# Gating the second pair of hardware loads on the first, and reordering the first software loads, in a windowed-attention plus feed-forward kernel

## The chip, the core and the metric

The kernel runs on one core of a Trainium2 chip. The metric is device time in microseconds (us) of one execution. Every kernel is executed several times and the median is quoted. One further execution is taken with the hardware profiler on; its times are counted in us from the start of the profiled span.

The engines are named as the profile names them: PE multiplies matrices, PEld is its loading of the stationary operand, DVE is the vector engine, ACT the scalar engine, POOL the general-purpose engine, SP the synchronisation engine. Each works through its own list of instructions in the order in which they were written. DMA transfers can be issued by SP and ACT ("hardware" queues q1 and q10 in the profile) and by POOL ("software" queue q0, the only one of the three that is used here to change float32 to bfloat16 on the way). All of them are carried out by the same 16 DMA engines.

## What is computed

The reference, cut to what matters: attention in a window of 32 positions to either side, over 8 batches, 8 heads, 576 positions and 64 columns per head, and behind it two matrix products with a squared ReLU between them.

```python
B, H, S, D = 8, 8, 576, 64
scores = np.matmul(q, k.transpose(0, 1, 3, 2)) / np.sqrt(D)
pos = np.arange(S)
mask = np.abs(pos[:, None] - pos[None, :]) <= 32
scores = np.where(mask, scores, -1e9)
scores = scores - np.max(scores, axis=-1, keepdims=True)
attn = np.exp(scores)
attn = attn / (np.sum(attn, axis=-1, keepdims=True) + 1e-09)
x = np.matmul(attn, v).transpose(0, 2, 1, 3).reshape(B * S, H * D)   # 4608 x 512
r = np.maximum(x @ w_in, 0.0)                                        # 4608 x 2048
out = (r * r) @ w_out                                                # 4608 x 512
```

## The kernel before

The work is cut into 72 attention steps of 64 tokens (nine per batch, numbered n) and nine feed-forward tiles of 512 tokens. For an attention step PE multiplies the keys around the 64 tokens with the queries (`scores`), ACT takes the exponential, DVE multiplies with the mask, PE multiplies with V (`av`), DVE divides by the sum (`evac`), and PE turns the result so that the columns lie on the partitions (`xturn`; later batches use a DMA transpose of SP for that). ACT copies the turned block into XT. When four groups of 128 tokens are there, the feed-forward of a tile can run: `mm1_small` and its larger relatives multiply with a quarter of the first weight (W1), ACT applies ReLU, DVE squares, and `mm2` multiplies with the second weight (W2).

**How the order comes about.** Nothing is issued directly. Every operation is recorded with the tags that it reads and writes, a planned duration, a `key` that serves as priority and, for a DMA, a planned amount of transfer (`move`). `schedule` then plans the five engines several times with a model of the engines and the DMA queues, keeps the plan with the best planned end, and `emit` writes each engine's instructions in that order with the semaphore waits that the tags ask for. An operation with a key of -100 or less keeps that key in every plan. A small change of keys or of planned transfer times therefore changes the written order of PE, DVE, ACT and SP far beyond the place of the edit.

**Loads at the start.** Batch 0 is loaded in six pieces of tokens, `PIECE0`: piece 0 has 96 tokens, piece 1 has 64, pieces 2, 3 and 4 have 128, piece 5 has 32. Pieces 0 and 2 of K and Q come in float32 through the hardware queues: `first_load`, line 454, K by SP and Q by ACT, into the borrowed buffers `oe` (piece 0) and `pf` (piece 2). Everything else comes through POOL and is turned to bfloat16 in flight: `tok_load` (line 461) for K and Q, `vx_load` (line 531) for V, `load_w1` and `load_w2` (lines 548 and 553) for the weights in quarters. In the string `ORDER`, k01 stands for piece 1 of K of batch 0, v00 for the first piece of V of batch 0, w10 for the first quarter of W1. The place in that string is the key, so the string is POOL's order.

**From a load to the first product.** `tok_turn` (line 489) turns a piece of K and Q on PE, and line 505 (DVE, K) and line 502 (ACT, Q) copy it to `kt` and `qt`. `vd_half` (line 543) makes a copy of V that is shifted by 64 tokens, on DVE. `scores` is line 585 on PE, line 605 on ACT and line 614 on DVE in batch 0; `av` is lines 720 and 721; `evac` is lines 731 and 733; `xturn` is line 749 on PE and 755 on ACT; the first feed-forward products of `mm1_small` are line 768 on PE, 776 on ACT and 824 on DVE.

**Warming products.** Until the planned end of the turn of piece 3, `fill` puts products of zeros (line 410) into the gaps that PE has in the plan, by the plan's count. They are ordinary instructions without a wait of their own and are executed in their place in the order, whether there is a gap or not.

The order in which `build` records the first loads of batch 0 before the change is this:

```python
if not b:
    for x in (0, 2):
        self.first_load("k", x, "SP", -300 + x)
        self.first_load("q", x, "ACT", -300 + x)
```

Of the kernel before, what the change touches and what calls it, by code (L numbers as in the profile page):

```python
# [30 lines left out]
PADS, MARGINS, ROUNDS, NREP = (0, 1000, 2000), (0, 4000, 8000), 3, 4  # L31
LATE = {"POOL": 1500, "SP": 2000, "ACT": 2000}
DEPTH, POST, BACK = 4000, {"POOL": 1500, "SP": 1000, "ACT": 1000}, {"POOL": 2500, "SP": 4000, "ACT": 4000}
ORDER = ("k01 q01 v00 v01 v02 w10 k03 q03 v03 k04 q04 v04 w11 w12 w13 k05 q05 k10 q10 v10 k11 q11 v11 "
         "w20 w21 w22 w23 k12 q12 v12 k13 q13 v13 k14 q14 v14").split()
GT0, WT0 = (12.5, 16, 20, 25.5), (13, 18, 23, 26)
TURN0 = {1: 1, 2: 2, 4: 3, 6: 4}
# [321 lines left out]
class Gen:  # L359
# [86 lines left out]
    def slot(self, b, x):  # L446
        return 512 * (x if b else x - 1)

    def first_load(self, t, x, eng, key):
        t0, n = PIECE0[x]  # L450
        src = (self.q if t == "q" else self.k)[0, :, t0:t0 + n, :].rearrange("h p d -> p h d")
        stg, o, w, tag = self.STG[t, x]
        dst = bass.AP(stg, o, [[w, n], [64, 8], [1, 64]])
        self.p.rec(eng, lambda e: e.dma_start(dst, src), writes=[tag], dma=(f"s{t}{x}", 0), key=key, dur=420, move=(n // 2, 14, 1500 if x == 0 else 2500))

    def tok_load(self, b, t, x, key):
        t0, n = self.pieces(b)[x]
# [88 lines left out]
    def load_w1(self, d, key):  # L546
        src = self.w_in[:, 512 * d:512 * d + 512].rearrange("(f p) c -> p f c", p=128)
        self.p.rec("POOL", lambda e: e.dma_start(self.W1[:, :, 512 * d:512 * d + 512], src),
                   writes=[("w1", d)], dma=(f"w1{d}", 0), key=key, dur=770, move=(32, 82 if d else 130, 500))

    def load_w2(self, d, key):
        src = self.w_out[512 * d:512 * d + 512, :].rearrange("(k p) c -> p k c", p=128)
# [342 lines left out]
    def build(self):  # L895
        p = self.p
        self.k1 = self.grp = 0
        self.group, self.bank = {}, {}

        K = -200.0  # L900
        self.setup_idle()
        self.setup_masks(K - 20)
        self.setup_rest(0, K + 3)
        self.setup_ptz(0, K + 2)
        self.setup_ptz(1, K + 2)
        self.setup_ptz(2, K + 2)
        self.setup_rest(1, -20)
        at = {it: K + 1 + k for k, it in enumerate(ORDER)}
        for d in range(4):
            self.load_w1(d, at[f"w1{d}"])  # L910
            self.load_w2(d, at[f"w2{d}"])

        tile = 0
        for b in range(B_):
            while 8 * tile + 7 < NCH * b:
                self.moe(tile)
                tile += 1
            if b < FB:
                if not b:
                    for x in (0, 2):  # L920
                        self.first_load("k", x, "SP", -300 + x)
                        self.first_load("q", x, "ACT", -300 + x)
                for bb in range(0 if b else FB):
                    for x in range(6):
                        for t in "kqv":
                            if f"{t}{bb}{x}" not in at:
                                continue
                            if t == "v":
                                self.vx_load(bb, x, at[f"v{bb}{x}"])
                            else:  # L930
                                self.tok_load(bb, t, x, at[f"{t}{bb}{x}"])
            else:
                for x in range(5):
                    kb = 9 * b - 40 + 2 * x
                    for t in "kq":
                        self.tok_load(b, t, x, kb)
                        self.dma_turn(b, t, x, 9 * b - LEAD - 9 + 2 * x)
                    self.vx_load(b, x, kb + 0.1)
            for c in range(NCH):
                n = NCH * b + c  # L940
                if b >= TB:
                    if c % 3 == 0:
                        if b == 1 and not c:
                            for x in range(2):
                                self.tok_turn(1, x, n - LEAD - 3)
                        self.scores(n, 3)
                        if c == 3:
                            self.vd_half(b, 1, 3, n - LEAD, [("sc", n)])
                        self.av3(n, 0)
                        self.av3(n, 1)  # L950
                        y = (n // 3) % 2
                        self.evac3(n, y)
                        if b == 1 and c < 6:
                            for x in range(2, 4) if not c else (4,):
                                if x < TX:
                                    self.tok_turn(1, x, n - LEAD)
                                else:
                                    for t in "kq":
                                        self.dma_turn(1, t, x, n - LEAD)
                        self.xturn3(n, y)  # L960
                    continue
                m = 1 if not c or n in (1, 8) else 2
                if n not in self.group:
                    if n == 0:
                        self.tok_turn(0, 0, -LEAD - 3)
                    if n == 8:
                        self.moe(0)
                        tile = 1
                        self.tok_turn(0, 5, -LEAD + 5)
                    self.scores(n, m)  # L970
                    if n + m < TB * NCH and n + m != 8:
                        bb, cc = divmod(n + m, NCH)
                        self.tok_turn(bb, (cc + 1) // 2 if bb else TURN0[cc], n + m - LEAD - 3)
                if c % 2 and not b:
                    x = (c + 1) // 2
                    self.vd_half(b, x - 1, x, n - LEAD - 3)
                if b and not self.group[n][1]:
                    odd = [c + u for u in range(self.group[n][2]) if (c + u) % 2]
                    if odd:
                        self.vd_half(b, odd[0] // 2, odd[-1] // 2 + 1, n - LEAD, [("sc", n)])  # L980
                self.av(n)
                gi, k, m = self.group[n]
                if n < 2:
                    self.evac(n, 1, 0, n)
                    if n:
                        self.xturn(0, 2, 0)
                elif k == m - 1:
                    self.evac(n - k, m, gi, 0)
                    self.xturn(n - k, m, gi)

        for T in range(tile, NT + 1):
            self.moe(T)
        p.schedule()
        with self.nc.Block():
            dsems, dcount = p.emit()
            for s in dsems:
                if s[0] == "o":
                    self.nc.sync.wait_ge(dsems[s], dcount[s])
# [32 lines left out]
```

The softmax here doesn't subtract the row's maximum and nothing guards it: scores larger than these inputs give would overflow.

## Time and profile before

| | value |
|---|---|
| median of 8 runs | 302.51 us (302.29 to 303.86) |
| the profiled execution: its own time | 303.86 us |
| its span | 302.0 us |
| its granted PE clock, mean | 0.994 |
| PE busy | 293.0 us, 97% of the span |
| DVE, ACT, POOL busy | 177.7, 159.9, 104.9 us |
| products of zeros, line 410 | 114 of them, 10.8 us |
| software queue q0 | 17.90 MB, 113,120 packets |
| hardware queues q1 and q10 | 11.15 and 9.83 MB |
| first feed-forward product, line 768 | starts at 16.94 us |

The page of a profile gives busy time by engine, a strip of 40 slices over the span, the DMA queues, the chain of work that ended last, and groups of instructions by source line. Beside the page, the trace answers questions about a stretch of time: a timeline of one engine, the busy time of an engine in given windows, and the packets of each DMA queue in a window. A line of the timeline has the start, the length, engine, line, operation and tiles; in brackets stands how long the engine was idle before it and what ended that. A DMA's time to landing is counted from the start of its issue to the update of its semaphore.

### The profile page before, as it was taken

The numbers are of one execution on the slowest core, as the hardware profiler recorded it, in microseconds if no ns is written. First come the engines' busy times: TensorE is split into PE (matmuls) and PEld (weight loads), VectorE is DVE, ScalarE is ACT, GpSimd is POOL, SyncE is SP. The second block draws the span as 40 slices with busy tenths as digits, with TensorE's granted clock in tenths as the row PEclk, the third lists the DMA queues.
The fourth block names the chain that finished last, engine by engine and source line by source line (L and its number), as shares of the span: only waits on it lengthen the run. The fifth ranks groups of instructions, "written<-read, shape, count | busy, mean of one in ns | idle before, by whom it ended". The sixth has DMA issues, their size and how long they took to land.

```text
span 302.0 us, 7047 instructions
## 1 busy us (share of the span) xinstructions
PE 293.0 (97%) x2760; PEld 173.7 (57%) x2796; DVE 177.7 (59%) x429; ACT 159.9 (53%) x267; POOL 104.9 (35%) x131
## 2 busy tenths in 40 slices
PE   8889999999999999999999999999999999999996
PEld 7779965775868764444444444444444444444445
DVE  5766656754998956658566496758448663222200
ACT  3357644574748645654565674647464654344411
POOL 8999732240604631552055544315410000000000
PEclk9799999999999999999999999999999999999999
DMA  9999999999999999999899999999992310000022
GB/s 146 173 195 170 206 172 173 156 168 164 179 142 124 139 165 166 144 136 144 164 116 119 149 185 158 124 173 89 172 162 63 96 26 35 37 35 36 35 82 94
DMA packets 166817, 39.34 MB, mean 130 GB/s; under 512 B 157824, under 2 KB 162304, under 8 KB 166784
## 3 DMA queue, kind: packets, MB, share of 16 engines
q0 software_dynamic: 113120, 17.90, 91.3%
q1 hardware_dynamic: 46512, 11.15, 23.7%
q10 hardware_dynamic: 7152, 9.83, 10.9%
q8 instruction: 22, 0.36, 0.5%
q14 instruction: 11, 0.09, 0.1%
HBM read 36.70 MB, written 9.44 MB: 153 GB/s over the span
## 4 chain that ended last, share of the span: by engine, by line
PE 93%; DVE 3%; DMA 2%; issue 1%; POOL 0%; POOLq 0%; DVEq 0%
PE outp L861 40%; PE ht L809 27%; PE ht L791 7%; PE ht L768 7%; PE sc L645 3%; PE sc L585 3%; DMA kraw<-in_k_dram 2%; DVE vd L543 2%; PE sc L489 1%; PE outp L410 1%; PE sc L837 1%; PE outp L837 1%; PE sc L693 0%; DVE kt L505 0%; PE sc L720 0%
## 5 line engine op out<-in xcount | busy, mean ns | idle before, releaser
L861 PE MATMUL outp<-w,gt 128*128 128x512 bf16 x534 | 131.6, 379 | 2.0 <-issue 1.0
L809 PE MATMUL ht<-xt,w 128*128 128x512 bf16 x374 | 93.2, 379 | 0.7 <-issue 0.3
L824 DVE TENSOR_TENSOR gt<-rt 128x512 bf16<-128x512 bf16 x144 | 59.2, 418 | 58.9 <-ACT rt L815 50.9
L815 ACT ACTIVATE rt<-ht 128x512 bf16<-128x512 f32 x96 | 57.3, 598 | 56.9 <-PE ht L809 54.0
L861 PEld LDWEIGHTS outp<-w,gt 128*128 128x128 bf16 x560 | 52.7, 98 | 58.2
L809 PEld LDWEIGHTS ht<-xt,w 128*128 128x128 bf16 x384 | 36.5, 98 | 42.4
L461 POOL DMA_DIRECT2D qraw<-in_q_dram x39 | 34.2, 876 | 51.6 <-PE ht L809 24.0
L461 POOL DMA_DIRECT2D kraw<-in_k_dram x39 | 34.5, 885 | 45.4 <-PE ht L809 19.5
L605 ACT ACTIVATE e<-sc 128x512 bf16<-128x512 f32 (+1 forms) x48 | 37.4, 808 | 12.1 <-PE sc L585 12.1
L531 POOL DMA_DIRECT2D vx<-in_v_dram x40 | 35.0, 875 | 19.9 <-PE ht L809 10.9
L868 ACT ACTIVATE oe<-outp 128x512 f32<-128x512 f32 x35 | 20.9, 598 | 26.5 <-PE outp L861 26.5
L669 DVE TENSOR_TENSOR xr<-pf,rs 128x512 bf16<-128x512 f32 (+1 forms) x42 | 27.7, 681 | 0.4
L626 DVE TENSOR_TENSOR pt<-e,mask 128x512 bf16<-128x512 bf16 x42 | 17.6, 421 | 14.0 <-ACT e L605 14.0
L768 PE MATMUL ht<-xt,w 128*128 128x128 bf16 x384 | 24.1, 219 | 0.3 <-ACT xt L755 0.3
L791 PE MATMUL ht<-xt,w 128*128 128x256 bf16 x192 | 23.5, 273 | 0.0
L768 PEld LDWEIGHTS ht<-xt,w 128*128 128x128 bf16 x384 | 21.7, 98 | 0.8 <-ACT xt L755 0.5
L662 DVE COPY pf<-sc 128x520 f32<-128x520 f32 x21 | 14.7, 699 | 11.5 <-PE sc L645 11.2
L791 PEld LDWEIGHTS ht<-xt,w 128*128 128x128 bf16 x192 | 18.0, 98 | 3.3
L776 ACT ACTIVATE rt<-ht 128x512 bf16<-128x512 f32 x24 | 14.2, 599 | 10.3 <-PE ht L768 10.0
L659 ACT ACTIVATE pf<-sc 128x520 f32<-128x520 f32 x21 | 12.6, 601 | 11.7 <-PE sc L645 11.7
L797 ACT ACTIVATE rt<-ht 128x512 bf16<-128x512 f32 x24 | 14.4, 599 | 7.4 <-PE ht L791 7.1
L664 DVE TENSOR_TENSOR pf<-pf 64x520 f32<-64x520 f32 x21 | 14.6, 697 | 5.6 <-ACT pf L659 4.7
(78 smaller groups left out, 197.3 us busy)
## 6 DMA issues: line engine op xcount, KB each, us to landing
out_dram<-oe ACTq DMA_DIRECT2D x35, 256.0 KB, 3.6
kraw<-in_k_dram POOLq DMA_DIRECT2D x30, 128.0 KB, 5.3
qraw<-in_q_dram POOLq DMA_DIRECT2D x30, 128.0 KB, 5.5
vx<-in_v_dram POOLq DMA_DIRECT2D x24, 128.0 KB, 5.4
w<-in_moe_w_in_dram POOLq DMA_DIRECT2D x4, 512.0 KB, 10.8
w<-in_moe_w_out_dram POOLq DMA_DIRECT2D x4, 512.0 KB, 17.2
vx<-in_v_dram POOLq DMA_DIRECT2D x16, 96.0 KB, 6.0
xt<-xr SPq DMA_TRANSPOSE x36, 4.2
```

The costliest lines, as they stand in the source:

```text
L461: self.p.rec("POOL", lambda e: e.dma_start(dst, src), writes=[("fraw", b, t, x)], old=[("fraw", b - 2, t, y + (b == 2))], reads=self.pace( ...
L531: self.p.rec("POOL", lambda e: e.dma_start(self.VX[b % 2][r:r + n, s, :, 0:64], self.v[b, :, t0:t0 + n, :].rearrange("h p d -> p h d")), w ...
L605: self.p.rec("ACT", lambda e, d=dst, a=src: e.activation(d, a, ACTF.Exp, scale=0.125), reads=["s" + x for x in name], writes=[("e", h)], k ...
L626: self.p.rec("DVE", lambda e, a=pt, c=ee, d=mb: e.tensor_tensor(a, c, d, ALU.mult), reads=[("e", k // 2), "mask"], writes=[("ptt", k)], ol ...
L669: self.p.rec("DVE", lambda e, w=w, np=np: e.tensor_tensor(bass.AP(self.XR, 512 * (2 * y + w), [[2048, np], [64, 2], [128, 4], [1, 64]]), b ...
L768: mm = e.matmul(ht[:, 128 * (d % 4):128 * (d % 4) + 128], self.W1[:, ft, 128 * d:128 * d + 128], self.XT[:, ft, t0:t0 + 128], start=(ft == ...
L791: mm = e.matmul(ht[:, 256 * (d % 2):256 * (d % 2) + 256], self.W1[:, ft, 128 * d:128 * d + 128], self.XT[:, ft, 64 * s0:64 * s0 + 256], st ...
L809: mm = e.matmul(ht[:], self.W1[:, ft, 128 * d:128 * d + 128], self.XT[:, ft, 512 * T:512 * T + 512], start=(ft == 0), stop=(ft == 3))
L815: self.p.rec("ACT", lambda e: e.activation(rt[:], ht[:], ACTF.Relu), reads=[("ht", k % 2)], writes=[("rt", k % 4)], key=key, dur=560)
L824: self.p.rec("DVE", lambda e: e.tensor_tensor(g, r, r, ALU.mult), reads=[("rt", k % 4)], writes=tags, key=key, dur=430)
L861: mm = e.matmul(op, gt[:, d, 128 * u:128 * u + 128], self.W2[:, d, :], start=(d == 0), stop=(d == 15))
L868: self.p.rec("ACT", lambda e: e.activation(oe[:], op, ACTF.Copy), reads=[tag], writes=[("oe", x % 4)], key=key, dur=560)
```

## The change

Four things are changed.

1. The second hardware loads, piece 2 of K on SP and piece 2 of Q on ACT, declare that they read the buffer that the first load of the same tensor writes. They don't use its data; the effect is a semaphore wait of SP, and of ACT, for the landing of piece 0 of K, and of Q.
2. They are recorded after the software loads of batches 0 and 1, with the keys -298 for both.
3. `ORDER` begins with v00 instead of k01 and q01, and the three pieces k03, q03 and v03 stand ahead of the first weight quarter w10 instead of behind it.
4. The planned transfer of w10 is 105 a packet group instead of 130. This changes nothing that is executed in itself; it is a number of the plan.

```diff
-ORDER = ("k01 q01 v00 v01 v02 w10 k03 q03 v03 k04 q04 v04 w11 w12 w13 k05 q05 k10 q10 v10 k11 q11 v11 "
+ORDER = ("v00 k01 q01 v01 v02 k03 q03 v03 w10 k04 q04 v04 w11 w12 w13 k05 q05 k10 q10 v10 k11 q11 v11 "
          "w20 w21 w22 w23 k12 q12 v12 k13 q13 v13 k14 q14 v14").split()
...
-    def first_load(self, t, x, eng, key):
+    def first_load(self, t, x, eng, key, gate=()):
...
-        self.p.rec(eng, lambda e: e.dma_start(dst, src), writes=[tag], dma=(f"s{t}{x}", 0), key=key, dur=420, move=(n // 2, 14, 1500 if x == 0 else 2500))
+        self.p.rec(eng, lambda e: e.dma_start(dst, src), reads=gate, writes=[tag], dma=(f"s{t}{x}", 0), key=key, dur=420, move=(n // 2, 14, 1500 if x == 0 else 2500))
...
-                   writes=[("w1", d)], dma=(f"w1{d}", 0), key=key, dur=770, move=(32, 82 if d else 130, 500))
+                   writes=[("w1", d)], dma=(f"w1{d}", 0), key=key, dur=770, move=(32, 82 if d else 105, 500))
...
                 if not b:
-                    for x in (0, 2):
-                        self.first_load("k", x, "SP", -300 + x)
-                        self.first_load("q", x, "ACT", -300 + x)
+                    self.first_load("k", 0, "SP", -300)
+                    self.first_load("q", 0, "ACT", -300)
...
+                if not b:
+                    self.first_load("k", 2, "SP", -298, [self.STG["k", 0][3]])
+                    self.first_load("q", 2, "ACT", -298, [self.STG["q", 0][3]])
```

The written order after the change, up to the first feed-forward product, for the engines that matter:

- POOL issues v00, k01, q01, v01, v02, k03, q03, v03, w10 and then as before.
- PE: turn of piece 0, turn of piece 1 (K, then Q), `scores` 0, 11 products of zeros, `scores` 1, `av` 0, 12 zeros, turn of K's piece 2, `av` 1, turn of Q's piece 2, 12 zeros, `xturn` of steps 0 and 1, `scores` 2 and 3, 7 zeros, turn of piece 3, `scores` 4 and 5, `av` 2 and 3, first product of line 768. There are 86 products of zeros in all. Before, it was: turn of piece 0, `scores` 0, turn of piece 1, turn of piece 2, `scores` 1, `av` 0, `scores` 2 and 3, `av` 1, `xturn`, `av` 2 and 3, first product of line 768, and only then the turn of piece 3.
- ACT: issue of Q's piece 0, issue of Q's piece 2 (now with the wait), loading of its function table, and then the copies of line 502.
- DVE: three shifted copies of V (line 543), for which v00 and v01 must have landed, now stand ahead of the first mask product (line 614), where there was none; seven instead of five stand ahead of the copy of K's piece 3 (line 505).
- From there on the lists of PE, DVE, ACT and SP differ from the former ones in many places over the whole run; POOL's list differs at two more places, in the loads of batch 2.

## The prediction

> **What bounds the kernel now.** I read the page first, then the busy time of PE in windows, then the chain of work that ended last, then the DMA queues packet by packet. PE is the bound:
>
> ```profile
> PE 293.0 (97%) x2760; PEld 173.7 (57%) x2796; DVE 177.7 (59%) x429; ACT 159.9 (53%) x267; POOL 104.9 (35%) x131
> ...
> PE 93%; DVE 3%; DMA 2%; issue 1%; POOL 0%; POOLq 0%; DVEq 0%
> ```
>
> The windows of PE (stretch, its length, PE busy, granted clock, DMA share, GB/s) show where it isn't doing useful work:
>
> ```profile
> 8.00:11.00 3.00, 2.78 (x26) 0.64 1.87 183
> ...
> 19.00:21.00 2.00, 1.19 (x29) 1.00 1.26 211
> ...
> 24.00:27.00 3.00, 3.00 (x65) 1.00 2.09 164
> ...
> 30.00:35.00 5.00, 5.00 (x100) 1.00 1.32 205
> ...
> 50.00:100.00 50.00, 49.47 (x616) 1.00 1.88 162
> ```
>
> From about 24 us on PE has no gap to speak of, so any delay of what is done by then goes straight to the end, and only what happens before can be won. As marker I take the end of `av` 7 with four blocks of line 768 behind it: 26.40 us in the chain, whose head is a load:
>
> ```profile
> 1.35 6.83 DMA kraw<-in_k_dram
> ...
> 8.22 0.29 PE sc L489 x4
> ...
> 9.11 0.87 PE ht L489 x4
> ...
> 17.11 0.89 PE ht L768 x16
> ...
> 26.40 1.79 PE ht L768 x32
> ```
>
> k01, the first software load, lands at 8.18 (1.35 + 6.83), q01 at 8.45 (2.15 + 6.3). The hardware loads, from the list of DMA issues (size, us to landing):
>
> ```profile
> pf<-in_k_dram SPq DMA_DIRECT2D x1, 256.0 KB, 5.6
> pf<-in_q_dram ACTq DMA_DIRECT2D x1, 256.0 KB, 6.7
> oe<-in_k_dram SPq DMA_DIRECT2D x1, 192.0 KB, 3.8
> oe<-in_q_dram ACTq DMA_DIRECT2D x1, 192.0 KB, 4.3
> ```
>
> Piece 0 is issued at 0.74, piece 2 at 1.19: landings 4.54 and 5.04, then 6.8 and 7.9. Now the question that decides: what were the queues doing meanwhile? Packets of a quarter of a microsecond at 5.25 us, and at 54.50 us:
>
> ```profile
> q10 hardware_dynamic: 166, 0.04, 107.8%
> q1 hardware_dynamic: 45, 0.01, 27.1%
> q0 software_dynamic: 9, 0.00, 7.0%
> ```
>
> ```profile
> q0 software_dynamic: 104, 0.01, 79.5%
> q1 hardware_dynamic: 99, 0.03, 76.1%
> ```
>
> No q0 packet exists before 5.25; then there are 9, 25, 50, 102, 136 in successive quarters. At 54.50, where q0 has a backlog and one hardware queue is active, the two take equal shares, some 205 packets a quarter together; q0 alone moves 306.
>
> **What the Trainium skill says.** "DMA: Bandwidth & Descriptors", Queues, rings and completion order: each DMA engine goes round-robin between the queues that have work. 104 against 99 agrees; so a ready q0 would have had a share at 3 to 5 us, and its zero there says that it was not ready. The same page, Specifications, gives a first byte of software DMA about 1 us after issue: k01 needs 3.9 (1.35 to 5.25), while the load issued at 118.48, with q0 idle, has its first packets at 119.9. The late start is a matter of the first use; no trace shows its cause. "TensorE: Matmul & The Clock Gate", Part 1: an idle window of about 3.4 us halves PE's clock, a busy one restores it. The trace agrees in kind: after the idle stretch at 7.1 to 8.2 the clock is 0.50 from 9.0 to 12.0, and zeros take 112 ns (34 in 3.81 us) against some 65 (15 in 1.00).
>
> **The gate.** SP waits for 4.54 and ACT for 5.04, then issue. Behind SP's wait stands nothing until its first transpose at 49.36. Behind ACT's wait stand the issue (0.65) and the table load (1.28), which now ends at about 7.0 instead of 3.15; the first copy of Q, at 6.00 before, comes 1 us later. I cost that at nothing, since k01's landing below is later still; without that cover it is 1.0 us. Issue to first packet was 1.0 (0.74 to 1.75), so the second loads start at 5.5 and 6.1, not at 3.6. The hardware queues are then empty from 4.0 to 5.5, and by the reading above q0 can't use that time.
>
> **When k01 and q01 land.** Packets are 256 B of source plus 16 for the semaphore: k01 and q01 528 each, v00 784, v01 and each 128-token piece 1040. v00 now goes first, so k01 is complete at q0's packet 1312 instead of 528. From 6.0 the engines owe 1312 - 84 of q0 (84 is what it had moved by 6.0 before) and 2080 - 250 of the hardware loads (half a microsecond of one queue at its 500 a us, an estimate).
> - Equal thirds at 820 a us: hardware 1830 / 547 = 3.3 us, to 9.3; q0 has 84 + 273 x 3.3 = 1000; the other 312 at 1220 take 0.3: 9.6.
> - q0 as weak as it was at 5.5 (25 of 211): hardware to 8.6, q0 then 340, the rest 0.8: 9.4.
> - Cheap mixing at 1220 a us in all: 3058 / 1220 = 2.5: 8.5.
>
> Before, k01's semaphore came 1.4 us after packet 528 (6.77, by adding up the windows), v01's 1.1 after packet 2880; with 1.3, k01 lands between 9.8 and 10.9. I take 10.5 and, 528 packets on, 10.9 for q01: 2.4 us later than before.
>
> **The walk of PE from there**, with before's durations. K turn 10.5, Q turn 10.9, `scores` 0 at 11.3, 11 zeros at the half clock (PE idles from 6.2 to 10.5) 1.2, `scores` 1 to 13.2. On DVE the first mask product stands behind two V copies (0.55 each) that wait for v01, at 11.8: ready at 13.3. `av` 0 to 14.1, 12 zeros 1.3 to 15.3, K's piece 2 (its load landed by 10) to 16.0, `av` 1 to 16.3, Q's piece 2 to 16.8, 12 zeros to 17.5. `xturn` waits for DVE's second division, 17.9; `scores` 2 and 3 to 18.5; 7 zeros; turn of piece 3 to 19.3. ACT now has four things in a row: XT copy 18.2 to 18.8, exponential (1.02) to 19.8, Q copy (0.6) to 20.4; so `scores` 4 and 5 run to 20.85, `av` 2 and 3 to 21.4, and the first line 768 starts at 21.4 against 16.94. Much of this is a change of order: piece 3 and `scores` 4 and 5, done at 20.7 before, are included. From 21.4: product 0.9, `xturn` of 2 and 3 at 22.5, `av` 4 and 5 to 23.7, turn of piece 4, product 24.1 to 25.0, `scores` 6 and 7, `xturn` 25.6, two products to 27.4, `av` 6 and 7, which wait for exponential and mask, to 28.1. Against 26.40: plus 1.7, and with some 0.1 for gaps as they fall, plus 1.8.
>
> Does anything give it back? q0 is about 2 us behind from here. w10 must land for the first product. It is now the last of the same nine loads, whose last, v03, landed at 16.1; plus 2 that is 18.1, used at 21.4, so moving three pieces ahead of it costs nothing; at an unshifted first product (16.94) it would have cost 1.2. w11 comes at 23 instead of 21.0, used at 25.6. The last quarter of W2 landed at 41.8 and is first used about 44.5; both move by the same 2. Later software loads are paced by PE. Everything after the marker is the same work in another order: nothing, with 0.3 either way.
>
> If the half clock ends at 12.4, as before, 12 zeros and a turn cost 0.9 less: plus 0.9. If k01 lands at 10.9: plus 2.3. At 9.8 with the fast clock: plus 0.5. **The sum:** span 302.0 + 1.8 = 303.8; the profiled execution took 303.86 in all, 1.86 around its span, and is the highest of the eight; on the median of 302.51 the same 1.8 gives 304.3.
>
> **Rivals.**
> - *The gate frees the software queue* (faster). It decides if q0 was held back by the hardware packets and starts when they end, at 4.0 or sooner. Then 1.5 us at up to 1220 carry v00 and most of k01 before the second loads come: k01 at 6.7, q01 at 7.8, and the walk's marker falls to 25.7: minus 0.7, 301.8. Starting at 3.0, all three land by 6.5, and the marker can fall to 24, where w11 (21.0) and the table load at 7.0 hold it: minus 2.4, 300.1. For it: not one packet of q0 in the whole time of the first loads. Against: equal shares at 54.50, and a start-up slope at 5.25 to 6.25 like that at 119.9 (16, 103, 105, 249), where there was no rival traffic. Middle 300.9.
> - *The loss is absorbed*. Before, PE ran 29 zeros between 16.3 and 18.8 and was 0.8 us idle from 19 to 21, while piece 3 had landed at 13.6 and 15.5. The new order uses that stretch. With the fast clock and k01 at 9.8 the rest is 0.5: 302.9.
> - *The gate doesn't do what it says*: the second loads' packets came behind the first ones anyway (q1 alone at 4.0: 211 packets to q10's 16), so the wait only inserts the 1.5 us from 4.0 to 5.5. That is inside my forecast, not another time.
>
> **Chances.** About 0.3% (0.9 us) is what a measurement of this kernel can tell from no change. Forecast, plus 0.9 to plus 2.9: 0.68, with its own range 303.4 to 305.3. Absorbed: 0.16, all within 0.3%. Freed: 0.16, of which 0.15 are faster by over 0.3%. So faster 0.15, same 0.17, slower 0.68. The range 301.4 to 305.4 leaves out most of the freed case and the tail above.
>
> **What would show it.** Right: hardware packets absent from 4.0 to 5.5, q0 still starting near 5.25, k01 landing at 9.8 to 10.9, PE idle before line 489 on kraw for some 4 us, first line 768 near 21.4, `av` 7 near 28. Wrong: q0 packets at 3 to 4 us and k01 landing before 8; or PE's clock back at full by 12.4 and line 768 before 20.

## The result and the profile after

The changed kernel took 305.0 us in the median of 11 runs, the kernel before 302.68 in the median of the 32 runs that it had by then: a ratio of 1.0076, with a 95% interval of 1.006 to 1.0093. One of the 11 took 438.14 us at a granted clock of 0.654; it stands in the median of 305.0 and in no other figure here. The profiled execution after took 304.67 us, with a span of 302.9 and a mean granted clock of 0.994.

Read in the order of the prediction. First, the page's line of busy time and the shares of the chain of work that ended last:

```profile
PE 291.6 (96%) x2734; PEld 172.1 (57%) x2768; DVE 176.7 (58%) x429; ACT 160.1 (53%) x267; POOL 104.7 (35%) x131
...
PE 87%; DVE 5%; DMA 4%; issue 2%; POOL 1%; ACT 1%; SPq 0%; DVEq 0%; POOLq 0%
```

PE has lost 6 points of the chain, and they went to DVE, to DMA and to stretches that wait for nothing shown. Where in time? The windows of PE (stretch, its length, PE busy, granted clock, DMA share, GB/s):

```profile
8.00:11.00 3.00, 0.53 (x11) 1.00 1.89 190
11.00:14.00 3.00, 2.04 (x22) 0.62 2.00 176
14.00:17.00 3.00, 3.00 (x50) 0.81 1.83 182
...
17.00:19.00 2.00, 1.16 (x27) 1.00 1.80 185
...
19.00:21.00 2.00, 1.87 (x49) 1.00 1.25 207
24.00:27.00 3.00, 3.00 (x64) 1.00 1.78 179
50.00:100.00 50.00, 49.53 (x644) 1.00 1.84 160
```

PE is nearly empty from 8 to 11, then works at a lowered clock until about 15. The 0.8 us that it was idle between 19 and 21 before have moved to the stretch from 17 to 19. From 24 on the windows shown hardly differ. The waits of PE between 4 and 20 us name one large one (engine, line, what it waited for: us, times, longest):

```profile
PE sc L720 <- DVE pt L614: 3.4, 1, 3.4
```

It isn't the wait that was forecast. Line 489 waits for no load at all; `av` 0 (line 720) waits for the first mask product. The chain tells what stands behind that product (start, length, what):

```profile
3.63 6.49 DMA vx<-in_v_dram
...
10.14 0.53 DVE vd L543
...
10.71 0.74 DVE vd L543
...
11.48 0.44 DVE pt L614
...
11.96 0.24 PE sc L720
...
12.58 1.28 PE outp L410 x12
13.86 0.85 PE ht L489 x4
...
26.54 2.68 PE ht L768 x48
```

v01 lands at 10.12 (3.63 + 6.49), two V copies follow, then the mask product, then PE. Its 12 zeros take 1.28 us, 107 ns each: the half clock. `av` 7 ends at 26.54, against 26.40 before.

So only 0.14 us of the 0.9 by which the span has grown are there at the marker. Most of the rest comes at one place far behind it, where `scores` waits for a DMA transpose (a line of PE's timeline: start, length, what, and in brackets the idle time ahead and what ended it); the profiled execution before has no such wait:

```profile
215.15 0.29 PE L585 MATMUL sc<-qt,kt 64*128 64x64 bf16 x8 [0.54 <-DMA qt<-qraw]
```

Piece 1 of K and of Q wasn't late, since the software queue started early. Packets from 3.25 to 3.50 us, and then from 3.75 to 4.00:

```profile
q10 hardware_dynamic: 215, 0.05, 96.1%
q1 hardware_dynamic: 38, 0.01, 15.8%
q0 software_dynamic: 11, 0.00, 8.7%
```

```profile
q0 software_dynamic: 119, 0.02, 94.9%
q10 hardware_dynamic: 35, 0.01, 16.3%
```

Before, q0's first packet came at 5.25; now it comes at 3.25. Both times that is the moment when one of the two hardware queues runs dry (q1: 45 packets before, 38 now). The DMA issues (size, us to landing) of k01, issued at 2.29, of q01 at 2.97, and of the two loads with the new wait, issued at 4.30 and 4.63:

```profile
kraw<-in_k_dram POOLq DMA_DIRECT2D x1, 64.0 KB, 3.6
qraw<-in_q_dram POOLq DMA_DIRECT2D x1, 64.0 KB, 3.4
pf<-in_k_dram SPq DMA_DIRECT2D x1, 256.0 KB, 6.6
pf<-in_q_dram ACTq DMA_DIRECT2D x1, 256.0 KB, 6.7
```

So k01 lands at 5.9 and q01 at 6.4, 2.3 and 2.1 us earlier than before, and the second hardware loads at 10.9 and 11.3 instead of 6.8 and 7.9.

One more thing is needed to read the medians. The mean granted clock of single executions takes three values: 1.0, 0.994 and 0.989. In the windows above, two stretches of 3 us at 0.62 and 0.81 lose 1.14 and 0.57 us, 1.71 together, which is what 3.4 us at half clock lose; 1.71 of 302.9 us is 0.0056. So the three values fit no, one and two such stretches. The kernel before, in 100 later executions on three chips, had 1.0 (two of them 0.999) in 91 and 0.994 in 9; the first 91 have a median of 302.31, the nine lie between 303.68 and 304.87. The execution whose profile stands before the prediction, 303.86 at 0.994, was one of that minority. The changed kernel, its profiled execution included, never had 1.0: 7 executions at 0.994, with a median of 304.67, and 4 at 0.989, with a median of 305.97.

### The profile page after: what moved, and what is told of

Its sections match the earlier page's. It is cut to its first block, busy times and chain, and to the rows that moved or that the text cites. A ratio compares the mean times of both kernels' runs of the same rounds, so it can differ in the third digit from the quotient of the medians.

```text
span 302.9 us, 6999 instructions
## 1 busy us (share of the span) xinstructions
PE 291.6 (96%) x2734; PEld 172.1 (57%) x2768; DVE 176.7 (58%) x429; ACT 160.1 (53%) x267; POOL 104.7 (35%) x131
## 3 DMA queue, kind: packets, MB, share of 16 engines
q10 hardware_dynamic: 7152, 9.83, 10.1%
## 4 chain that ended last, share of the span: by engine, by line
PE 87%; DVE 5%; DMA 4%; issue 2%; POOL 1%; ACT 1%; SPq 0%; DVEq 0%; POOLq 0%
PE outp L861 38%; PE ht L809 26%; PE ht L768 7%; PE ht L791 5%; PE sc L585 3%; PE sc L645 3%; DMA qt<-qraw 2%; DMA vx<-in_v_dram 2%; PE sc L489 1%; DVE gt L824 1%; PE outp L410 1%; DVE pf L664 1%; DVE pf L662 1%; DVE xr L669 1%; DVE vd L543 1%
## 5 line engine op out<-in xcount | busy, mean ns | idle before, releaser
L861 PE MATMUL outp<-w,gt 128*128 128x512 bf16 x533 | 133.0, 379 | 2.1 <-issue 1.0
L809 PE MATMUL ht<-xt,w 128*128 128x512 bf16 x377 | 95.4, 379 | 0.6 <-issue 0.3
L662 DVE COPY pf<-sc 128x520 f32<-128x520 f32 x21 | 14.7, 698 | 12.5 <-PE sc L645 12.4
```

Source lines behind the costliest of these rows:

```text
L662: self.p.rec("DVE", lambda e, d=dst, c=src: e.tensor_copy(d, c), reads=["sA", "sC"], writes=[("pf", 0)], key=key, dur=610, att=True)
L809: mm = e.matmul(ht[:], self.W1[:, ft, 128 * d:128 * d + 128], self.XT[:, ft, 512 * T:512 * T + 512], start=(ft == 0), stop=(ft == 3))
L861: mm = e.matmul(op, gt[:, d, 128 * u:128 * u + 128], self.W2[:, d, :], start=(d == 0), stop=(d == 15))
```

## The experiments

All are one program with switches. With the switches as in the first line it issues what the changed kernel issues; each experiment's diff is against that line, except where it says so.

```python
PLAN, GATE, LOADS, MASK_FIRST, CUT = "new", True, "new", False, 0
ZEROS, DROP = {}, ()
```

PLAN says whose written order of PE, ACT, DVE and SP is used, GATE whether the two waits are there, LOADS whose order POOL's first nine loads have. MASK_FIRST and CUT are told where they are used, ZEROS and DROP add and take out products of zeros. Every kernel computes the whole output. Behind "Measured" stand the median, its ratio to the kernel before, measured beside it on the same chip (302.31 to 302.33 on each of the three chips), and the 95% interval of that ratio; then how often each clock came. The first three versions and the old order after 45 us ran on one chip, the next four on a second, the last four on a third; which chip the first measurement of the changed kernel had isn't on record.

The theories: A, the loss lies in the first 20 us, where PE stands idle and the granted clock then falls; B, it lies in the later part of the new written order; C, the two waits by themselves are all of it. D came up later: the lowered clock itself is the loss, not the landings.

### The waits alone

```diff
-PLAN, GATE, LOADS, MASK_FIRST, CUT = "new", True, "new", False, 0
+PLAN, GATE, LOADS, MASK_FIRST, CUT = "old", True, "old", False, 0
```

> The kernel before with its own written order on every engine, its own order of loads (k01 first), and only the two waits added to it. Theory A (the gate does free the software queue, but the second hardware loads then land near 11 and everything behind them waits): k01 lands near 5.5 instead of 8.2, PE stands at the turn of piece 2 until about 11 instead of 8.9, first line 768 at about 19 instead of 16.9, and the run is 1.5 to 2 us slower than before. Theory B (the time is lost by the new written order of the whole run, the gate costs nothing): within 0.3% of before.

Measured: 305.55, ratio 1.0081 (1.0048 to 1.0114); 5 executions at 0.989, 4 at 0.994. PE's waits before 20 us in the profiled execution, which was the slowest of the nine (308.38):

```profile
PE ht L494 <- DMA pf<-in_q_dram: 3.0, 1, 3.0
PE ht L494 <- DMA pf<-in_k_dram: 2.3, 1, 2.3
```

In the old order piece 2 is turned ahead of `av` 0, and now its loads are last (10.8 and 14.5 us). The waits alone cost 3.2 us, more than the whole change and more than the 1.5 to 2 of theory A; the first product is at 21.5, not at 19. They don't have to be the change's whole loss: the new order puts the turn of piece 2 later and avoids these two waits.

### All but the waits

```diff
-PLAN, GATE, LOADS, MASK_FIRST, CUT = "new", True, "new", False, 0
+PLAN, GATE, LOADS, MASK_FIRST, CUT = "new", False, "new", False, 0
```

> The changed kernel with its written order on every engine and its new order of loads, only the two waits taken out. Theory A (gate and new order each cost about as much at the start): the software queue starts near 5.2 again, v00, k01 and q01 land at 8 to 9, v01 near 10 as in the changed kernel, the V copies and the first mask product come at the same time, and the total is within 0.5 us of the changed kernel. Theory C (the gate is the loss): back to the time before, 2 us faster than the changed kernel.

Measured: 304.09, 1.0039 (1.0024 to 1.0053); 10 at 0.989, 12 at 0.994, none at 1.0. q0 is late again (v00 lands at 8.1, k01 at 8.6), and PE waits for it, again with nothing to do ahead:

```profile
PE sc L494 <- DMA kraw<-in_k_dram: 2.7, 1, 2.7
```

C falls: without its waits the change still loses 0.4%. Theory A's half microsecond isn't met either: the median is 0.9 us below that of the first measurement of the changed kernel, and 0.4 below that of the second (304.52, further down). From `av` 0 on (it starts at 11.82 here and at 11.96 in the changed kernel) the two profiled executions run within 0.3 us of each other; different waits lead to the same place.

### The V copies behind the mask products

MASK_FIRST moves the two V copies on DVE that wait for v01 from ahead of the first mask product to behind the first division.

```diff
-PLAN, GATE, LOADS, MASK_FIRST, CUT = "new", True, "new", False, 0
+PLAN, GATE, LOADS, MASK_FIRST, CUT = "new", True, "new", True, 0
```

> The changed kernel with one edit on DVE: the two shifted V copies that wait for v01 stand behind the first two mask products and the first division, not ahead of the first mask product. Theory A (these two copies hold PE idle from 8.6 to 12.0 and bring on the half clock): av 0 at about 8.6, the turn of K's piece 2 at about 11 when its load lands, first line 768 near 18, where w10 lands (17.8) and becomes the bound, and 1.5 to 2 us faster than the changed kernel, about 303.2. Theory B (the written order of the rest of the run is the loss): no faster than the changed kernel by more than 0.5.

Measured: 303.59, 1.0031 (1.0014 to 1.0047), the first to beat the changed kernel with the waits in. `av` 0 starts at 8.6; the 3.4 us become three waits of 1.2 (K's second load), 1.1 and 1.1 (DVE). 14 of 22 executions have the clock at 1.0, with a median of 303.27. So the mask product behind v01 is what held PE, and splitting the idle time is worth about 1 us (303.59 against 304.52 on another chip; 305.0 at first).

### The old order after 45 us

CUT keeps the new order up to a planned 45 us and takes the old one from there on.

```diff
-PLAN, GATE, LOADS, MASK_FIRST, CUT = "new", True, "new", False, 0
+PLAN, GATE, LOADS, MASK_FIRST, CUT = "new", True, "new", False, 45000
```

> The changed kernel up to the planned time of 45 us, and from there on every engine in the written order of the kernel before. Theory B (0.8 us of the difference come after 27 us, 0.5 of them at 215 us, where scores waits for a DMA transpose): 0.5 to 0.8 us faster than the changed kernel, and no such wait. Theory A (the start is all of it): within 0.3 us of the changed kernel.

Measured: 304.83, 1.0055 (1.0037 to 1.0074); 304.01 at 0.994, 305.04 at 0.989. No wait for a DMA transpose is left. To compare by clock, the changed kernel was run once more, on the second chip:

> The changed kernel itself, so that it stands beside the next three on the same chip. As measured, about 305.0, clock 0.994 or 0.989 in every execution. If the chip makes a difference, it is at about 304.2, beside the version without the gate (304.1).

Measured: 304.52, 1.007 (1.0051 to 1.0089); 304.05 at 0.994 and 305.11 at 0.989. These medians and those of the old tail agree within 0.1 at each clock. That doesn't dispose of B, for the two ran on different chips, and against the first measurement of the changed kernel (304.67 and 305.97) the old tail is 0.66 and 0.93 faster, as B had it. The traces say what B is worth. The wait at 215 us is there in the first profiled execution of the changed kernel (0.5 us) and in two versions with the same late order, the one without the waits (0.6) and the one with the V copies moved (1.3). It isn't there in the second profiled execution of the changed kernel, which falls no further behind after 20 us than the one with the old tail. So the new late order costs 0.5 us or more in some executions and nothing in others; why, no run shows. The 2.2 us that the changed kernel loses on the second chip don't need it.

### Zeros in the gap

56 products of zeros ahead of `av` 0: they add work to PE and fill the 3.4 us.

```diff
-ZEROS, DROP = {}, ()
+ZEROS, DROP = {"av0": 56}, ()
```

> The changed kernel with 56 more products of zeros ahead of av 0, in the gap in which PE waits for the mask product; nothing else is changed. Theory D (the clock is the loss: the gap of 3.4 us puts PE at half speed for one or two stretches of 3.4 us, in every execution of the changed kernel and in few of the kernel before): the granted clock is 1.0 in most executions and the time falls by 1 to 2 us, to 303 to 304. Theory A (the landings are the loss, PE has to wait for them whatever its clock): within 0.4 of the changed kernel.

Measured: 303.73, 1.0041 (1.0025 to 1.0057), all six executions at 1.0. PE's windows in the changed kernel, and then with the zeros (columns as above):

```profile
8.00:12.00 4.00, 0.57 (x12) 0.97 2.03 181
12.00:16.00 4.00, 4.00 (x46) 0.61 1.69 190
```

```profile
8.00:12.00 4.00, 3.57 (x66) 1.00 2.00 177
12.00:16.00 4.00, 3.63 (x70) 1.00 1.71 187
```

From 12 to 16 PE needed all of 4.00 us for 46 products at 0.61; now it does 70 in 3.63. More work ahead of the same wait makes the kernel 0.8 us faster than the changed kernel on the same chip (304.52), a little less than the 1 to 2 us of theory D. The first line 768 is at 18.78 instead of 19.79. Beside the second profiled execution of the changed kernel (0.989, span 303.3), the one with the zeros is 2.2 us ahead where ScalarE takes the exponential at 18.38 instead of 20.57, and 1.3 us ahead from about 32 us to the end (302.0): some 0.9 us of what the filled gap gave is lost again in between. What that is comes below.

The reverse, in the kernel before, with no load moved: the 12 zeros between its turns of Q's piece 0 and K's piece 1 are taken out.

```diff
-PLAN, GATE, LOADS, MASK_FIRST, CUT = "new", True, "new", False, 0
-ZEROS, DROP = {}, ()
+PLAN, GATE, LOADS, MASK_FIRST, CUT = "old", False, "old", False, 0
+ZEROS, DROP = {}, (("qturn00", "kturn01"),)
```

> The kernel before without the 12 products of zeros between the turn of Q's piece 0 and the turn of piece 1; loads, gate and order as before. Theory D: PE is now idle for most of the stretch from 6 to 8.2 us, the clock is 0.994 or lower in most executions, and the kernel is 1.5 to 2.5 us slower than before with the loads exactly where they were. Theory A: within 0.3 us of before, since no load moves.

Measured: 303.40, 1.0031 (1.0017 to 1.0044). No execution of eight is at 1.0 any more, where 19 of 21 of the kernel before on that chip were. Less work, 1.1 us more; theory D had 1.5 to 2.5.

### No waits, and zeros in the gap

```diff
-PLAN, GATE, LOADS, MASK_FIRST, CUT = "new", True, "new", False, 0
-ZEROS, DROP = {}, ()
+PLAN, GATE, LOADS, MASK_FIRST, CUT = "new", False, "new", False, 0
+ZEROS, DROP = {"kturn01": 44}, ()
```

> The changed kernel without the two waits, with 44 more products of zeros ahead of the turn of K's piece 1, for which PE otherwise stands 2.7 us. Theory D: clock 1.0 in most executions and 1 to 2 us faster than the version without the gate (304.1), about at the time of the kernel before. Theory A: unchanged, 304.1.

Measured: 302.34, 0.9992 (0.9978 to 1.0006), all 14 executions at 1.0. The new order of work and loads costs nothing once the gap ahead of K's piece 1 is filled; unfilled it was 304.09 (on another chip, where before had the same median). With the waits and the gap filled it was 303.73: so 1.4 us of the loss stays that isn't the half clock. The remaining runs ask about these 1.4.

### What is left at the full clock

First the landing of the second weight quarter (theory L), which is 22.8 with waits and zeros and 20.8 with zeros alone. `"w11"` is the new order of loads with w11 ahead of k04, q04 and v04.

```diff
-PLAN, GATE, LOADS, MASK_FIRST, CUT = "new", True, "new", False, 0
-ZEROS, DROP = {}, ()
+PLAN, GATE, LOADS, MASK_FIRST, CUT = "new", True, "w11", False, 0
+ZEROS, DROP = {"av0": 56}, ()
```

> The changed kernel with 56 products of zeros ahead of av 0, as before (303.7, all at the full clock), and the second weight quarter w11 moved up ahead of the pieces k04, q04 and v04 in the software queue. Theory L: what the wait still costs at the full clock (303.7 against 302.3 without it) is the software queue running about 2 us later, so that the second weight quarter (landing at 22.8 instead of 20.8) is late for the first dense products; then moving it up by 2.2 us of issue brings 302.4 to 302.9. Theory I: it is the short gaps in the middle of groups of dense products, which end on nothing that the profile shows (0.4, 0.15 and 0.4 us between 23 and 31 us), and no landing; then 303.5 to 304.0 again.

Measured: 304.21, 1.0066 (1.0043 to 1.0089), six executions at 1.0. Moving the load up didn't help: L falls. The run is slower by 0.5 us, which neither theory expected; that the move did it isn't shown, for in its profiled execution v01, which stands ahead of everything moved, already lands at 10.6 instead of 9.9.

Then fewer zeros (44 ahead of `av` 0):

```diff
-ZEROS, DROP = {}, ()
+ZEROS, DROP = {"av0": 44}, ()
```

> The changed kernel with 44 instead of 56 products of zeros ahead of av 0: they fill 2.6 us of the 3.4 us and leave 0.8 us bare. Theory L (the late second weight quarter): 303.5 to 304.0 again, since no load moves. Theory I (gaps in the supply of TensorE's instructions, where 56 more of them sit ahead): the gaps move or go, and the time comes out elsewhere, 302.3 to 303.2. If the bare 0.8 us is enough for a half-clock stretch, there are clocks of 0.994 among the executions and 304 or more.

Measured: 303.43, 1.0042 (1.0023 to 1.006), 9 executions at 1.0 or 0.999. That lies between the two expectations and decides little by itself; its trace says more. Its first line 768 is at 18.83, 0.15 us behind the kernel without waits (18.68). After that PE has one gap in a group that waits for no semaphore (the timeline; in brackets the idle time ahead and what ended it):

```profile
31.32 0.20 PE L594 MATMUL sc<-qt,kt 64*128 64x64 bf16 x1 [0.42 <-issue]
```

The list of queues has one that carries instructions. Between 28.80 and 28.85 us one packet of it starts:

```profile
q8 instruction: 1, 0.02, 117.0%
```

Of such gaps there are two with 56 zeros (0.15 and 0.41 us; PE resumes at 23.83 and 31.04) and one with w11 moved up (0.54 us; 25.15); the packet before each starts at 21.45, 28.6 and 22.7. Together with 31.32 and 28.80: PE resumes 2.35 to 2.5 us after the start of the packet in all four. The page "Runtime: NRT & Kernel Launch" of the Trainium skill, Instruction fetch mechanics, says that each engine refills its instructions in blocks of 16 KiB by a queue of its own and that the cost is mostly hidden; the packet of 0.02 MB agrees. That PE waited for this block is argued from the four pairs of times; if so, the cost isn't hidden here, but shows with 0.42 us. The kernel with zeros and no waits has its packet just before 28.0 and no gap. Beside that kernel, the one with 56 zeros starts the same ReLU on ScalarE 0.3 us later at 25.4 and 0.9 us later at 31.5, and 0.9 later to the end: its two gaps are where nearly all of the difference between the two profiled executions comes.

Does that gap come from the waits? The same kernel without waits, with 44 zeros ahead of K's piece 1, and with MASK_FIRST, was tried as a version to beat both:

```diff
-PLAN, GATE, LOADS, MASK_FIRST, CUT = "new", True, "new", False, 0
-ZEROS, DROP = {}, ()
+PLAN, GATE, LOADS, MASK_FIRST, CUT = "new", False, "new", True, 0
+ZEROS, DROP = {"kturn01": 44}, ()
```

> An attempt at a faster kernel: the changed order of work and loads without the waits, 44 products of zeros ahead of K's second turn, and VectorE's two V copies behind the first two mask products. The run with the same zeros and the V copies where they were took 302.34 at the full clock and waited 0.8 us for the mask product ahead of av 0. If that wait sets the time: 301.4 to 301.9. If the chain through ScalarE's Q copy (0.8 us wait ahead of the scores of step 2) sets it whatever comes before: 302.2 to 302.5. If the earlier av 0 only makes room for a wait on the next load: 302.2 to 303, with more waiting for loads ahead of the second turn.

Measured: 304.28, 1.0053 (1.0035 to 1.0071), 8 of 10 executions at 1.0. It beats nothing. The wait for the mask product is gone, and one of 1.4 us for DVE's division takes its place ahead of `xturn`, so that line 768 starts at 18.80. The gap is there as well, 0.42 us, PE resuming at 31.29, with the packet at 28.8. So the gap doesn't need the waits. Of the 0.8 us between the spans of the run with 44 zeros and waits (301.9) and the run with zeros alone (301.1), 0.15 lie ahead of line 768. The rest comes at this gap: ScalarE is 0.15 us later up to 30.8 us, and 0.65 to 0.8 later from 32.5 to the end.

### The loads alone

```diff
-PLAN, GATE, LOADS, MASK_FIRST, CUT = "new", True, "new", False, 0
+PLAN, GATE, LOADS, MASK_FIRST, CUT = "old", False, "new", False, 0
```

> The kernel before with its own written order on every engine, without the waits, and with only the software queue's loads in the changed order (v00, k01, q01, v01, v02, k03, q03, v03, then w10). Theory that the reorder is nearly free: k01 and q01 land some 0.4 us later (v00's 96 KB ahead of them), the first weight quarter 2 to 2.5 us later and still ahead of its first product at about 17; 302.3 to 303.0, with more executions at a clock of 0.994 than before, since the gap ahead of K's second turn grows. Theory that the reorder carries a large part of the loss: 303.7 or more, as in the run without the waits that also had the changed order (304.1).

Measured: 303.74, 1.0043 (1.003 to 1.0057): 4 executions at 1.0 (303.31), 5 at 0.994 (303.76), 2 at 0.989. The wait for k01 grows from 1.1 to 1.4 us, and the clock falls in more executions, as expected. But the four at 1.0 are 1.0 us above before too, and its profiled execution (0.994) runs within 0.1 us of the one of before (0.994), by ScalarE's instructions, from 21 us to the end. So no trace here shows that microsecond. The kernel before has it in 24 of its 91 executions at the full clock (303.25 to 303.30, against 302.3), but in none of the 22 on the chip of this run. What it is stays open.

## Why the number came out and the way to it didn't

**The gate: "the hardware queues are then empty from 4.0 to 5.5, and by the reading above q0 can't use that time".** This step failed. q0 starts at 3.25, and it has 180 packets in the quarter after 4.0. The reading took equal shares at 54.50 for a rule and concluded that q0 wasn't ready before 5.25. The runs show the other thing: without the waits q0 is late (v00 at 8.1), with them it is early (5.5). The equal turns that the Trainium skill's "DMA: Bandwidth & Descriptors", Queues, rings and completion order, lets one expect between queues with work are not seen at the start: in both kernels q0 moved nothing while both hardware queues were backed up. Whether q0 got no turn or had no packets ready isn't settled. The rival *the gate frees the software queue* had this right: it gave k01 at 6.7, or all three loads by 6.5 if q0 started at 3.0; measured are 5.9 and 6.4.

**k01 at 10.5, PE idle for 4 us ahead of line 489.** It fell with the first step. PE was idle for 3.4 us all the same, at 8.6 instead of 6.2, for another reason: the walk had the two V copies behind v01, "at 11.8: ready at 13.3", but took v01 to be late by as much as k01. k01 came 4.6 us before its forecast, v01 only 1.7 (at 10.1), and so the mask product, ready at 11.9, alone was the last to come. The freed rival overlooked the same: its marker at 25.7 or 24 left v01 and DVE out.

**The walk: line 768 at 21.4, `av` 7 at 28.1, plus 1.8.** Measured 19.79 and 26.54: plus 0.14. Between `av` 0 and line 768 the new order went as written (turn, zeros, `xturn`, `scores` 4 and 5 behind ScalarE's Q copy), 1.5 us earlier.

**The sum.** Here one error met another, and that the number came out is luck. The shift was worked out against a profiled execution with a half-clock stretch in it, at 0.994, and then added to the median of executions of which most had none. At equal clocks the changed kernel loses next to nothing (304.05 and 304.67 at 0.994, against 303.68 to 304.87, median 304.80, before). What changed is how often PE is slowed: in 9 executions in 100 before, in all after. How much of the 2.3 us between the medians that is, the runs don't agree on: nearly all by this comparison at equal clocks, 0.8 us by the filled gap, since the kernel with the filled gap loses time elsewhere. The forecast's 1.8 held 0.9 for a half clock that lasts longer, "if the half clock ends at 12.4, as before"; in most executions of before there was none to end. The Trainium skill's "TensorE: Matmul & The Clock Gate", Part 1, calls the window of some 3.4 us free-running, so that the same gap can be counted or not. That agrees with the clock of one kernel taking different values. The page also asks for a whole idle window, and there the measurement differs: PE idle for 1.1 us was counted in 9 of 100, for 3.4 in every one.

**Landings and the table load.** The second loads land at 10.9 and 11.3 and are used at 13.86 and later: hidden, as forecast. The table load ends at 6.35 (7.0 in the forecast), and the first Q copy comes at 6.37 (6.00 before); PE's wait for v01 covers that as well. w10 lands at 17.8 and is used at 19.8: nothing, as forecast.

**"Everything after the marker is the same work in another order: nothing, with 0.3 either way".** Held in part. In the first profiled execution the new order lost some 0.7 us behind the marker, most of it at the wait at 215 us; in the second it lost nothing that the old tail doesn't lose.

Shown: an idle gap ahead of `av` 0, made by v01 and DVE's order, lowers the clock, and filling it gives back 0.8 us. Also shown: the new orders without waits cost nothing with the gap filled. Not settled: the other 1.4 us between 303.73 and 302.34. Of these the two profiled executions (303.85 and 302.88) show 0.9: some 0.1 comes before the first product and the rest at the two gaps that look like late instructions. Such a gap also came without the waits (the run of 304.28), so the waits aren't shown to cause it; every gap of this kind, with a packet some 2.4 us ahead of its end, stands in a kernel with added zeros. More instructions may put the end of a block elsewhere; no run tests that. What remains, and the full microsecond between executions of equal clock, no trace explains.

## What to carry to other kernels

Before a shift is added to a median, look at the clock of every execution: a profiled execution may be of a kind that the median isn't, and then a gap that costs nothing in the chain can move the median by a microsecond by making the rare kind the rule. Where a load is freed, ask which load the next engine waits for in its written order: k01 came 2.3 us earlier and v01, behind it in the queue and ahead of the mask product on DVE, kept PE idle. In this kernel a gap that couldn't be closed was better filled or split than left whole, though the filling had a price further on.

## What was not expected of the hardware

- Two backed-up hardware queues left the software queue without a packet until 5.25 us, and until 3.25 where they were held back; at 54.50, against one hardware queue, it had half.
- The two hardware loads of 256 KB took 6.6 and 6.7 us beside a running software queue, and 5.6 and 6.7 when they went first. In the run with the waits alone, Q's took 9.5.
- 56 more products made a kernel 0.8 us faster; 12 fewer made one 1.1 us slower.
- TensorE stood for 0.42 us inside a group that waits for no semaphore, and went on 2.5 us after its 16 KB packet of instructions began; in four such cases the distance was 2.35 to 2.5 us.
- The same program waited 0.5 us for a DMA transpose at 215 us in one profiled execution and not at all in another.
